# Attention and two expert layers: groups of 512 and 256 tokens in place of 384 and 384 at the start

## The chip, the cores and the metric

One core of a Trainium2 chip. The metric is device time of one execution in microseconds; the kernel before takes 1459.46 us (median of 3 runs, 1459.11 to 1459.53).

## The reference, cut to what matters

```python
# attention: 8 batches x 8 heads x 576 tokens x 64; keys and values pooled by 8 -> 72
k_p = k.reshape(B, H, Sp, 8, D).mean(axis=3)
v_p = v.reshape(B, H, Sp, 8, D).mean(axis=3)
attn = softmax(scale * q @ k_p.T)                  # float32
x = (attn @ v_p) as [4608 tokens, 512]
h = x @ w_in                                       # 512 -> 2048
x2 = (h * cos(h)) @ w_out                          # 2048 -> 512
logits = x2 @ w_gate                               # 8 experts, the best one alone
out[mask_e] = gate * (relu(x2[mask_e] @ w1[e]) @ w2[e])
```

## The kernel before

The 4608 tokens go through attention and the first dense layer in 12 groups (`NG`) of 384 tokens (`GT`), three tiles of 128; then the routed experts follow, which the change leaves alone but for one load. A group g has 16 steps s, one for each 128 of the 2048 hidden features:

- `mm1(s)` (L394): 12 matmuls of 384 columns into one of two banks HB (x and w_in are each a high and a low part: high x high, low x high, high x low). x of the group lies in xTh, xTl.
- `chain_a(s)`: ScalarE scales (L402) and rounds into the bank RB (L403); VectorE takes the rest of the division by 2 pi (L405, a bank and `tA` as inputs); ScalarE takes the sine (L406). `chain_b(s)`: VectorE multiplies with h from its bank (L411), ScalarE copies the high part gh (L412), POOL forms the low part gl (L413).
- `mm2(s)` (L420): 9 matmuls of 512 columns, three for each tile, summed over s in the three banks ACC. It runs two steps late, behind mm1(s+2). mm2(15) stands behind mm1(0) of the next group, and there `evac` copies the three sums to x2t (L425 to L427) and stores them to `x2d` (L429, three DMAs on SP).

Group 0 also decodes the weights, which arrive as raw 64-bit numbers: for each step `w_load` (two DMAs of 512 KB), `w_scale` (two ScalarE operations, L514), `w_bits` (six VectorE operations of 128x512, L519 to L521, through two rotating banks), `w_parts` (two ScalarE casts L526, two POOL subtractions L527), all some steps ahead. In the opening, before the loop, the keys and values of batch 0 are pooled (`pool_k` L313, `pool_v` L324), the three tiles of group 0 get their `scores` (L335, L342 to L348, softmax weights), `norm` (L355 to L358, the last on POOL), `transp` (L365, copies L369 and L371) and `pv` (L382, high part L385 on ScalarE, low part L386 on VectorE), and the first decodes run.

Each later group's attention is hung on the steps of the group before it, by `at(step, function)`: a score at steps 1, 5, 9 (in group 0 at 9, 12, 13), its transposes three steps later, the four pv at the end. So are the pooling of keys and values for the next batch (`load_k`, `pool_k`, `load_v`, `pool_v`), the queries' load two groups ahead (`load_q`, L303, 768 KB), and from group 1 on the routing: 24 `route_dot` (L452) of VectorE for each group on the evacuated x2t, spread over steps 1 to 11, then `route_sel`, `route_pos`, `route_put`.

Nothing is reordered: each engine and each DMA queue works its instructions in the order of the program, and semaphores make it wait. The order within a step of groups 1 to 10 is

```python
mm1(s)
if s == 0: mm2(15)
if s >= 2: mm2(s - 2)
chain_a(s)
if s == 0: evac(g - 1)
route_dot(...)
chain_b(s)
route_dot(...)
for f in ex[s]: f()     # scores, norm, transp, pool_k, load_q, ...
```

and in group 0 the decode of step s+3 stands inside `chain_a(s)`, between L403 and L405, with `chain_b(s-1)` after its second operation.

## Time and profile before

| | |
|---|---|
| median of 3 runs | 1459.46 us |
| profiled execution, its time | 1458.9 us |
| profiled execution, its span | 1457.1 us |
| TensorE busy | 1406.2 us (97%) |
| VectorE, ScalarE, POOL busy | 878.0, 736.3, 442.9 us (60%, 51%, 30%) |
| mm1(0) of group 0, of group 1, of group 2 starts | 32.14, 127.93, 204.87 us |
| TensorE's idle time before L394, ended by VectorE's L411 | 4.8 us in all |

The span runs from the first instruction to the last of the profiled execution; its time holds 1.8 us more. Rows of a timeline give start, duration, engine, line, what is written and read, and in brackets how long the engine was idle before and what ended that. A matmul's duration in a timeline is longer than the distance between two, since they overlap; the distance is what counts. A row of busy time by stretch gives the stretch, then its length and, for PE, PEld (TensorE's weight loads), DVE, ACT and POOL, the busy microseconds with the count of instructions, then the granted clock of TensorE (1.00 being full speed), the share of the DMA engines and their GB/s. DVE is VectorE, ACT ScalarE.

### The profile page before, as it was taken

To read this page: it belongs to the slowest core of one execution; us is meant where nothing else is said; L and a number is where in the kernel's file an instruction comes from. 1 tells how busy PE (TensorE), PEld (TensorE's weight loads), DVE (VectorE), ACT (ScalarE), POOL (GpSimd) and SP (SyncE) were. 2 spreads that over 40 slices of the span, in tenths; PEclk is the share of its full clock that TensorE was granted. 3 is DMA by queue.
4 is the path that set the end of the run, shared out by engine and by line. 5 is a ranking of instruction groups with operands and counts; after the bars stand their busy time and mean duration, and the time that the engine had idled before them with its cause. 6 is when DMAs were issued, how large, how long until landed. Compare 5 with 4: busy or idle time off the path is not lost. (4 is left out here: it accounts for less than half of the span.)

```text
span 1457.1 us, 23304 instructions
## 1 busy us (share of the span) xinstructions
PE 1406.2 (97%) x8295; PEld 1219.2 (84%) x8295; DVE 878.0 (60%) x1949; ACT 736.3 (51%) x1353; POOL 442.9 (30%) x421
## 2 busy tenths in 40 slices
...
GB/s 301 201 149 110 63 47 63 38 2 22 71 39 63 47 23 22 55 55 39 63 30 23 22 1 82 59 37 211 213 233 210 146 156 157 32 44 42 59 30 32
DMA packets 42692, 119.94 MB, mean 82 GB/s; under 512 B 6179, under 2 KB 22179, under 8 KB 39856
## 3 DMA queue, kind: packets, MB, share of 16 engines
...
## 5 line engine op out<-in xcount | busy, mean ns | idle before, releaser
L394 PE MATMUL bank<-xh,WI 128*128 128x384 f32 x1536 | 436.5, 345 | 6.5 <-DVE tA L411 4.8
L420 PE MATMUL bank<-wb,gh 128*128 128x512 f32 x1152 | 395.8, 398 | 0.0
L394 PEld LDWEIGHTS bank<-xh,WI 128*128 128x128 f32 x1536 | 284.6, 190 | 19.5 <-DVE tA L411 7.0
L420 PEld LDWEIGHTS bank<-wb,gh 128*128 128x128 f32 x1152 | 217.2, 189 | 53.5 <-issue 5.3
L394 PE MATMUL bank<-xl,WI 128*128 128x384 f32 x768 | 260.9, 340 | 0.2 <-DVE xl L386 0.2
L420 PE MATMUL bank<-wb,gl 128*128 128x512 f32 x576 | 228.3, 396 | 0.3 <-POOL gl L413 0.2
L807 PEld LDWEIGHTS bank<-E,wb 128*128 128x128 f32 x1632 | 208.7, 191 | 20.0 <-issue 7.4
L807 PE MATMUL bank<-E,wb 128*128 128x256 f32 x1632 | 213.9, 283 | 5.3 <-DVE xh L811 2.5
L452 DVE SCALAR_TENSOR_TENSOR E<-x2t,wgb 128x512 bf16<-128x512 f32 x264 | 216.6, 820 | 2.1
L817 PE MATMUL bank<-wb,xh 128*128 128x512 f32 x816 | 209.5, 395 | 0.0
L810 ACT ACTIVATE xh<-bank 128x256 fp32r<-128x256 f32 x136 | 52.2, 384 | 293.8 <-PE bank L807 293.8
L811 DVE SCALAR_TENSOR_TENSOR xh<-bank,xh 128x256 fp32r<-128x256 f32 x136 | 57.5, 424 | 217.3 <-ACTq L995 96.5
L413 POOL TENSOR_TENSOR gl<-tA,gh 128x384 fp32r<-128x384 f32 x96 | 107.7, 1122 | 252.5 <-ACT gh L412 245.9
L413 POOL TENSOR_TENSOR gl<-E,gh 128x384 fp32r<-128x384 f32 x96 | 105.3, 1097 | 260.3 <-ACT gh L412 224.1
L817 PEld LDWEIGHTS bank<-wb,xh 128*128 128x128 f32 x816 | 145.5, 189 | 25.4 <-issue 0.2
L394 PEld LDWEIGHTS bank<-xl,WI 128*128 128x128 f32 x768 | 146.5, 191 | 4.8 <-DVE xl L386 0.5
L196 POOL DMA_INDIRECT E<-x2d,E x44 | 46.1, 1048 | 271.2 <-PE bank L631 256.8
L420 PEld LDWEIGHTS bank<-wb,gl 128*128 128x128 f32 x576 | 108.6, 189 | 18.6 <-POOL gl L413 1.0
L405 DVE SCALAR_TENSOR_TENSOR tA<-bank,tA 128x384 f32<-128x384 f32 x96 | 52.8, 550 | 77.9 <-ACT bank L403 77.9
L405 DVE SCALAR_TENSOR_TENSOR E<-bank,E 128x384 f32<-128x384 f32 x96 | 53.1, 553 | 61.7 <-ACT bank L403 61.6
L406 ACT ACTIVATE E<-E 128x384 f32<-128x384 f32 x96 | 50.4, 525 | 72.3 <-DVE E L405 72.0
L402 ACT ACTIVATE tA<-bank,consts 128x384 f32<-128x384 f32 x96 | 55.1, 574 | 52.0 <-PE bank L394 52.0
...
## 6 DMA issues: line engine op xcount, KB each, us to landing
...
```

The source lines that it names most:

```text
L196: POOL.indirect_dma_start(out=xg[i], out_offset=None, in_=x2d[0:n], in_offset=bass.IndirectOffsetOnAxis(ap=column(u, i)[0], axis=0), bound ...
L394: PE.matmul(o, lhsT=a, rhs=x[:, c], start=n == 0, stop=n == 11)
L402: ACT.activation(a, h, AF.Identity, scale=INV2PI, bias=consts[:, C_TP + 1:C_TP + 2])
L405: DVE.scalar_tensor_tensor(a, r, MAGIC, a, op0=ALU.subtract, op1=ALU.subtract)
L406: ACT.activation(a, a, AF.Sin, scale=-TWOPI)
L413: POOL.tensor_tensor(gl[s % 2], a, gh[s % 2].bitcast(F32), op=ALU.subtract)
L420: PE.matmul(ACC[i], lhsT=a[:, sl], rhs=w_tile(s)[:, DM * w:DM * w + DM], start=s == 0 and n == 0, stop=s == NCH - 1 and n == 2)
L452: DVE.scalar_tensor_tensor(junk, x2[i], 1.0, wgb[:, DM * e:DM * e + DM], op0=ALU.mult, op1=ALU.mult, accum_out=lgs[:, i, e:e + 1])
L807: PE.matmul(o, lhsT=w_tile(4 * w + s // 2)[:, f], rhs=x[:, c], start=n == 0, stop=n == 11)
L810: ACT.activation(h, o, AF.Relu)
L811: DVE.scalar_tensor_tensor(l, o, 0.0, h.bitcast(F32), op0=ALU.max, op1=ALU.subtract)
L817: PE.matmul(OP[i], lhsT=a[s % 3][:, 128 * i:128 * i + 128], rhs=w_piece(w, s), start=s == 0 and n == 0, stop=s == 7 and n == 2)
```

## The change

Group 0 takes four tiles (512 tokens) and group 1 two (256); the others keep three. `WIDTH`, `BEGIN` and `TILES` replace `GT` where a group's tokens are counted. What follows from it:

- the fourth sum of group 0 goes to the bank ROT[0], and waits there until the end of group 1: `evac(0)` takes three tiles, `evac(1)` takes ROT[0] and group 1's two. The rotating banks are RB and ROT[1] in group 0, ACC[2] and ROT[1] in group 1;
- the rounding of chain_a goes in group 0 to SBUF (`kin`), no longer to the bank RB, since that bank rotates;
- x of group 0 (channel block 3), and gl of odd steps, lie in a new tile X0; its place is taken later by QF, the queries of group 2 and on. So `load_q(2)` stands in group 1, step 0, behind `evac(0)`; `load_q(1)` moves from the opening to group 0, step 4;
- group 0's queries and softmax weights use weight places and EF; the opening has a fourth score, norm and transp; the four `pv(0, c)` all stand ahead of `w_scale(2)` and `w_bits(2)`, no longer between its operations;
- one score and two transposes fewer stand in group 0; the pooling of values for batch 2 (`load_v`, `pool_v`) moves from group 1, steps 5 to 14, to group 2, steps 0 to 5;
- the first expert's w1 is loaded in two DMAs (EF and QF).

```diff
+BEGIN = [0, GT + TP] + [GT * g for g in range(2, NT // GT + 1)]
+WIDTH = [b - a for a, b in zip(BEGIN, BEGIN[1:])]
+TILES = [w // TP for w in WIDTH]
...
+    X0 = ep.tile([128, 4 * GT], F32R, name="X0", tag="e2")
+    Q0 = [w_tmp(i) for i in range(2)] + [EF[:, 2 * W0 * i:2 * W0 * i + 2 * W0] for i in range(3)] + [w_tmp(2)]
...
+    def xT(g, k, c):
+        t, w = (xTh, xTl)[k].rearrange("p c t -> p (c t)"), WIDTH[g]
+        if g == 0 and c == 3:
+            return X0[:, W0 * k:W0 * k + W0]
+        return t[:, w * c:w * c + w]
...
+    def gx(g, k, p):
+        w = WIDTH[g]
+        if g == 0:
+            return X0[:, 2 * W0:] if k and p else GB[:, W0 * (2 * p + k):W0 * (2 * p + k) + W0]
...
+    def accs(g):
+        return ACC + ROT[0:1] if g == 0 else ACC[0:TILES[g]]
...
-    def chain_a(s, meanwhile=lambda: None):
-        h, r = HB[s % 2][:, 0:GT], RB[:, 0:GT]
-        a = tA[s % 2]
+    def chain_a(g, s, meanwhile=lambda: None):
+        h, a = HB[s % 2][:, 0:WIDTH[g]], tA(g, s % 2)
+        r = kin[:, 0:W0] if g == 0 else RB[:, 0:WIDTH[g]]
...
     def evac(g):
         for i in range(3):
+            acc = (ROT[0:1] + ACC if g == 1 else ACC)[i]
...
     w_load(4)
-    pv(0, 0)
+    for c in range(4):
+        pv(0, c)
     w_scale(2)
-    w_bits(2, {2 * i: lambda i=i: pv(0, i) for i in (1, 2)})
-    pv(0, 3)
+    w_bits(2)
     w_parts(1)
...
-            for i in range(3):
+            for i in range(TILES[g + 1]):
                 if g == 0:
-                    at((9, 12, 13)[i], scores, 3 * (g + 1) + i, i)
-                    at((9, 12, 13)[i], norm, i)
-                    if i < 2:
-                        at((11, 14)[i], transp, i)
+                    at((9, 12)[i], scores, g + 1, i)
+                    at((9, 12)[i], norm, i)
+                    at((11, 14)[i], transp, g + 1, i)
...
-            if g + 2 < NG:
-                at(10 if g > 0 else 14, load_q, g + 2)
+            if 0 < g < NG - 2:
+                at(10, load_q, g + 2)
+            if g == 0:
+                at(4, load_q, 1)
...
+        if g == 2:
+            for c in range(4):
+                at((0, 2, 3, 5)[c], pool_v, 2, c)
+                if c < 3:
+                    at((0, 2, 3)[c], load_v, 2, c + 1)
...
             if s == 0 and g > 0:
                 evac(g - 1)
+                if g < 3:
+                    rbanks[:] = [ACC[2], ROT[1]] if g == 1 else ROT
+                if g == 1:
+                    QF.append(ep.tile([128, 4 * GT], F32, name="QF", tag="e2"))
+                    load_q(2)
```

The order of the instructions at three places. **VectorE in the opening**, from the end of the second decode on; before, L386 is pv's subtraction and L519 to L521 are the decode:

```order
L521 SCALAR_TENSOR_TENSOR tmp_157<-wgb,bank_85 128x512
L386 TENSOR_TENSOR xl<-bank_78,xh 128x384
L519 TENSOR_SCALAR bank_79<-tmp_155 128x512
L519 TENSOR_SCALAR bank_80<-tmp_156 128x512
L386 TENSOR_TENSOR xl<-bank_81,xh 128x384
L520 SCALAR_TENSOR_TENSOR bank_79<-tmp_155,bank_79 128x512
L520 SCALAR_TENSOR_TENSOR bank_80<-tmp_156,bank_80 128x512
L386 TENSOR_TENSOR xl<-bank_82,xh 128x384
```

In the changed kernel (L433 is the subtraction, L565 to L567 the decode):

```order
L567 SCALAR_TENSOR_TENSOR tmp_160<-wgb,bank_79 128x512
L433 TENSOR_TENSOR xl<-bank_80,xh 128x512
L433 TENSOR_TENSOR xl<-bank_81,xh 128x512
L433 TENSOR_TENSOR xl<-bank_82,xh 128x512
L433 TENSOR_TENSOR X_108<-bank_83,X_108 128x512
L565 TENSOR_SCALAR bank_84<-tmp_157 128x512
L565 TENSOR_SCALAR bank_85<-tmp_158 128x512
```

The four subtractions, spread through the decode before, stand in a row ahead of it.

**SP at the start of group 1**, before (L303 loads queries, L765 the gate weights, L429 stores the evacuated tiles, L309 and L319 load keys and values):

```order
L319 DMA wgb<-vP 72x1024 x4
L303 DMA early<-qT 128x4x384
L765 DMA wgb<-wgt 128x4096
L429 DMA x2d<-x2t 128x512 x3
L309 DMA E_71<-kT 128x576 x3
```

In the changed kernel (L343, L827, L475 and L349 are the same loads and stores):

```order
L359 DMA wgb<-vP 72x1024 x4
L827 DMA wgb<-wgt 128x4096
L475 DMA x2d<-x2t 128x512 x3
L343 DMA QF<-qT 128x4x384
L349 DMA E_71<-kT 128x576 x4
```

The queries of group 2 move from ahead of the gate weights to behind the three stores.

**VectorE in group 2**, step 2 of the changed kernel to L456 of step 3 (L450 and L456 are L405 and L411 of before, L498 the dots, L364 pool_v, L353 pool_k):

```order
L450 SCALAR_TENSOR_TENSOR TA<-bank_83,TA 128x384
L498 SCALAR_TENSOR_TENSOR E_72,lgs<-x2t,wgb 128x512
L456 TENSOR_TENSOR TA<-bank_78,TA 128x384
L498 SCALAR_TENSOR_TENSOR E_72,lgs<-x2t,wgb 128x512 x2
L522 TENSOR_REDUCE st_117<-sm_114 128x3
L523 TENSOR_SCALAR st_117<-st_117 128x3
L524 RECIPROCAL pay<-st_117 128x3
L364 TENSOR_REDUCE E_71<-E_71 72x128
L353 TENSOR_REDUCE E_71<-E_71 128x72
L450 SCALAR_TENSOR_TENSOR E_72<-bank_83,E_72 128x384
L498 SCALAR_TENSOR_TENSOR E_72,lgs<-x2t,wgb 128x512
L456 TENSOR_TENSOR E_72<-bank_79,E_72 128x384
```

The L364 row is new there; the other rows stand as they did.

## Rows read from the trace of the kernel before

**Rows 1.** Busy time by stretch, three stretches of groups 0 and 1.

```profile
43.00:46.00 3.00, 3.00 (x10) 3.00 (x11) 3.00 (x6) 2.88 (x6) 2.54 (x3) 0.50 0.13 31
50.00:60.00 10.00, 10.00 (x53) 9.20 (x52) 10.00 (x19) 9.63 (x19) 8.01 (x8) 1.00 0.60 210
128.00:205.00 77.00, 77.00 (x427) 66.67 (x428) 58.73 (x133) 48.55 (x83) 21.51 (x19) 1.00 0.16 52
```

**Rows 2.** Timeline of TensorE, group 0 and the start of group 1.

```profile
42.83 0.69 PE L394 MATMUL bank<-xh,WI 128*128 128x384 f32 x1 [4.50 <-DVE tA L411]
...
82.39 0.44 PE L335 MATMUL bank<-E,early 64*128 64x72 f32 x2 [2.25 <-DVE x2t L521]
...
127.93 0.44 PE L394 MATMUL bank<-xh,WI 128*128 128x384 f32 x1
```

**Rows 3.** Timeline of TensorE, one full step of group 0 at full speed.

```profile
53.93 0.34 PE L394 MATMUL bank<-xh,WI 128*128 128x384 f32 x1
...
56.02 0.39 PE L420 MATMUL bank<-wb,gh 128*128 128x512 f32 x1
...
58.11 0.34 PE L394 MATMUL bank<-xh,WI 128*128 128x384 f32 x1
```

**Rows 4.** Timeline of TensorE, 256-wide matmuls in the experts' part.

```profile
1013.66 1.59 PE L807 MATMUL bank<-E,wb 128*128 128x256 f32 x12
...
1015.09 1.55 PE L817 MATMUL bank<-wb,xh 128*128 128x512 f32 x6
```

**Rows 5.** Timeline of ScalarE, one head's exponential of a score in the opening.

```profile
12.87 0.32 ACT L348 ACTIVATE att<-bank,mxs 128x72 f32<-128x72 f32 x1
```

**Rows 6.** Timeline of VectorE, opening: decodes of weights and pv's subtractions.

```profile
22.72 1.27 DVE L519 TENSOR_SCALAR bank<-wgb 128x512 uint32<-128x512 uint32 x2
...
30.05 0.55 DVE L386 TENSOR_TENSOR xl<-bank,xh 128x384 fp32r<-128x384 f32 x1
...
35.66 1.29 DVE L519 TENSOR_SCALAR bank<-wgb 128x512 uint32<-128x512 uint32 x2
```

**Rows 7.** Timeline of TensorE, opening: pv of group 0.

```profile
26.82 5.39 PE L382 MATMUL bank<-early,E 72*64 72x384 f32 x16
```

**Rows 8.** Timeline of VectorE, group 0: L405 of two neighbouring steps.

```profile
50.91 0.55 DVE L405 SCALAR_TENSOR_TENSOR tA<-bank,tA 128x384 f32<-128x384 f32 x1
...
55.42 0.55 DVE L405 SCALAR_TENSOR_TENSOR E<-bank,E 128x384 f32<-128x384 f32 x1
```

**Rows 9.** Timeline of SP's queue, group 1: stores of group 0, load of queries.

```profile
133.27 1.31 SPq L429 DMA_DIRECT2D x2d<-x2t  x3
...
173.34 0.38 SPq L303 DMA_DIRECT2D early<-qT  x1
```

**Rows 10.** Busy time by stretch: the load's last bytes (last two columns).

```profile
176.00:178.00 2.00, 2.00 (x11) 1.68 (x10) 1.93 (x5) 1.95 (x3) 0.72 (x1) 1.00 0.63 237
```

**Rows 11.** Timeline of VectorE, group 1.

```profile
137.42 0.45 DVE L342 TENSOR_REDUCE mxs<-bank 128x4 f32<-128x288 f32 x1
...
141.65 1.47 DVE L452 SCALAR_TENSOR_TENSOR E<-x2t,wgb 128x512 bf16<-128x512 f32 x1
...
143.53 0.67 DVE L452 SCALAR_TENSOR_TENSOR E<-x2t,wgb 128x512 bf16<-128x512 f32 x1
...
164.89 1.21 DVE L324 TENSOR_REDUCE E<-E 72x128 f32<-72x1024 f32 x1
...
185.59 0.08 DVE L452 DVE_READ_ACCUMULATOR E<-x2t,wgb 128x1 f32 x1
```

**Rows 12.** Timeline of VectorE, group 2.

```profile
208.46 0.56 DVE L405 SCALAR_TENSOR_TENSOR tA<-bank,tA 128x384 f32<-128x384 f32 x1 [4.05 <-ACT bank L403]
...
219.96 0.56 DVE L411 TENSOR_TENSOR tA<-bank,tA 128x384 f32<-128x384 f32 x1
```

**Rows 13.** Timeline of TensorE, group 2: mm1(4).

```profile
220.75 0.34 PE L394 MATMUL bank<-xh,WI 128*128 128x384 f32 x1
```

**Rows 14.** Timeline of POOL, group 0: one of the weights' low parts.

```profile
50.20 1.30 POOL L527 TENSOR_TENSOR WI<-tmp,WI 128x512 fp32r<-128x512 f32 x1
```

More of the change, by code (lines that the diff above doesn't have):

```diff
@@ L241, in split @@
             if isinstance(st, int):
-                s = EF if half == 0 else wgb
+                s = wgb if half else QF[0] if c > 5 else EF
             else:
@@ L376, in pv, with mm1 @@
             hh = 2 * c + h
[L377 to L378 removed]
+            t = BEGIN[g]
+            while t < BEGIN[g + 1]:
                 b = t // S
[L380 to L381 removed]
+                e = min((b + 1) * S, BEGIN[g + 1])
+                sl = slice(t - BEGIN[g], e - BEGIN[g])
                 PE.matmul(o[64 * h:64 * h + 64, sl], lhsT=vp[b % 2][:, hh * D:hh * D + D],
[L383 removed]
+                          rhs=attnT(g, hh)[:, sl], start=True, stop=True)
                 t = e
[L385 to L389 removed]
+        h, l, o = xT(g, 0, c), xT(g, 1, c), o[:, 0:WIDTH[g]]
+        ACT.copy(h, o)
+        DVE.tensor_tensor(l, o, h.bitcast(F32), op=ALU.subtract)
+    def mm1(g, s):
+        o = HB[s % 2][:, 0:WIDTH[g]]
         n = 0
@@ L406, in chain_a, with chain_b, mm2 @@
         ACT.activation(a, a, AF.Sin, scale=-TWOPI)
-    def chain_b(s):
-        h = HB[s % 2][:, 0:GT]
-        a = tA[s % 2]
-        DVE.tensor_tensor(a, h, a, op=ALU.mult)
-        ACT.copy(gh[s % 2], a)
-        POOL.tensor_tensor(gl[s % 2], a, gh[s % 2].bitcast(F32), op=ALU.subtract)
-    def mm2(s):
-        h, l = gh[s % 2], gl[s % 2]
-        for i in range(3):
+    def chain_b(g, s):
+        o, a = HB[s % 2][:, 0:WIDTH[g]], tA(g, s % 2)
+        h, l = (gx(g, k, s % 2) for k in range(2))
+        DVE.tensor_tensor(a, o, a, op=ALU.mult)
+        ACT.copy(h, a)
+        POOL.tensor_tensor(l, a, h.bitcast(F32), op=ALU.subtract)
+    def mm2(g, s):
+        h, l = (gx(g, k, s % 2) for k in range(2))
+        for i, acc in enumerate(accs(g)):
             sl = slice(i * TP, i * TP + TP)
             for n, (a, w) in enumerate(((h, 0), (l, 0), (h, 1))):
-                PE.matmul(ACC[i], lhsT=a[:, sl], rhs=w_tile(s)[:, DM * w:DM * w + DM], start=s == 0 and n == 0, stop=s == NCH - 1 and n == 2)
+                PE.matmul(acc, lhsT=a[:, sl], rhs=w_tile(s)[:, DM * w:DM * w + DM], start=s == 0 and n == 0, stop=s == NCH - 1 and n == 2)
     def evac(g):
         for i in range(3):
+            acc = (ROT[0:1] + ACC if g == 1 else ACC)[i]
             if i == 1:
-                DVE.tensor_copy(x2[i], ACC[i])
+                DVE.tensor_copy(x2[i], acc)
             else:
-                ACT.copy(x2[i], ACC[i])
+                ACT.copy(x2[i], acc)
             r = (3 * g + i) * TP
@@ L568, in w_parts @@
                 p.parts()
[L570 removed]
+    seed = TA[:, 0:288].rearrange("p (r two) -> p r two", two=2)
     POOL.memset(seed[:, :, 0], SENT)
@@ L575, in attention_moe_kernel @@
         load_k(0, c)
-    for i in range(3):
-        t = slice(i * TP, i * TP + TP)
-        SP.dma_start(out=qs[:, :, t], in_=qT[:, :, t].rearrange("c p t -> p c t"))
+    for t in (slice(0, TP), slice(TP, W0)):
+        for i in range(2):
+            SP.dma_start(out=Q0[i].rearrange("p (c t) -> p c t", c=2)[:, :, t], in_=qT[2 * i:2 * i + 2, :, t].rearrange("c p t -> p c t"))
     for c in range(4):
@@ L594, in attention_moe_kernel @@
     pool_v(0, 0)
-    scores(1, 1, True)
+    scores(0, 1, True)
     norm(0, True)
     pool_v(0, 1)
-    scores(2, 2)
+    scores(0, 2)
     norm(1, True)
+    scores(0, 3, True)
+    w_scale(0)
     norm(2)
-    w_scale(0)
+    norm(3, True)
     pool_v(0, 2)
```

143 lines of the change are left out of this document (79 added, 64 removed).

## Prediction

> **What bounds the kernel now.** I read the busy time by stretch first, then the timelines of the stretches that the change touches. In group 1 TensorE is busy 77.00 us of 77.00 and VectorE 58.73; in the middle of group 0 VectorE is busy without a gap, 10.00 of 10.00 [rows 1]. So the fourth tile is put where VectorE is the limit, and taken from where TensorE is. A microsecond that TensorE waits in the short group is paid in full; the room in group 0 is what TensorE now loses there. Its timeline shows that: a wait of 4.50 us before mm1(2) at 42.83, one of 2.25 at 82.39 [rows 2], and smaller ones up to the group's end. Behind the first the granted clock is 0.50, the lower of the two levels, from 43 to 46 us and on [rows 1].
>
> **Widths.** Twelve 384-wide matmuls of mm1 take 2.09 us (53.93 to 56.02) and nine of mm2 as long (to 58.11): 4.18 a step [rows 3], 0.174 and 0.233 each. Twelve 256-wide ones elsewhere take 1.43 (1013.66 to 1015.09), 0.119 each [rows 4]. mm2's matmuls are 512 wide, so mm1's at 512 get their 0.233. A step then costs TensorE 12 x 0.233 + 12 x 0.233 = 5.59 with four tiles and 12 x 0.119 + 6 x 0.233 = 2.83 with two. 192 x (0.233 + 0.119 - 2 x 0.174) = 0.8 us more than 384 twice; it is inside the steps below.
>
> **Opening.** The fourth tile needs its softmax before the loop: eight exponentials on ScalarE of 0.3, 2.4 us [rows 5]; on VectorE two more maxima and three small operations, about 1.0, and 1.5 of waiting for ScalarE. The first weight decode, at 22.72 [rows 6], starts near 25.2 and ends at 28.9. The fourth tile's transposes use its banks, so the last of their copies end near 31.1. pv's 16 matmuls take 5.39 us for 384 columns [rows 7]; by proportion 7.2 at 512, and I take 6.9: until 38.0. Before, VectorE's four subtractions L386 stood between the operations of decode 2, and it never waited: the first at 30.05, decode 3 at 35.66 [rows 6]. Now all four stand ahead of decode 2, each behind its pv; the last ends near 39.35, decode 2 takes 3.6 (35.66 - 30.05 less four L386 of 0.47, as before), and decode 3 starts at 43.0. From there to mm1(2) it was 7.2 us (35.66 to 42.83: the decode, L405, two pool_k, two operations of decode 4, L411); with 512 columns 0.2 more. mm1(2) starts at 50.4, not 42.83: **+7.5**. Bounds: pv at full speed, 16 x 0.233 = 3.7, leaves +4.3; a collision of VectorE with POOL adds 0.7.
>
> **Rest of group 0.** VectorE repeats every 4.51 us (50.91 to 55.42) [rows 8]: six decode operations, 3.58, and two of 0.47. At 512 columns those two come to about 0.6 each: 4.78, under TensorE's 5.59. So TensorE becomes the limit and its waits from 82 us on go; the one before mm1(2) stays, and with it the slow stretch, which lost half of 5.8 us, 2.9. Counted forward on TensorE: 14 steps of 5.59 are 78.3; mm2(14) 2.8; the slow stretch 2.9. Scores, transposes and pv of a group of three are what group 1 has over its steps, 77.0 - 16 x 4.18 = 10.1; of two tiles, 6.7. What is late next: transposes at step 11 want a bank that a decode still holds, about 1.5, and mm2(14) its last gl, about 0.7. Together 92.9, where 85.1 stood (42.83 to 127.93 [rows 2]): +7.8, for a tile that adds 14 x (5.59 - 4.18) = 19.7. Group 1 begins at 50.4 + 92.9, say 143.
>
> **Group 1, two tiles.** Two things hold it. First, the queries of group 2. Their new place is that of x and gl of group 0, free only after mm2(0,15), and the load stands on SP behind the three stores of the evacuation. Their issue ended at 133.27 + 1.31 = 134.6 [rows 9], 4.6 after mm1(0) (127.93 + 2.09). With narrower ScalarE operations ahead of it I take 4.0: 143 + 1.43 + 4.0 = 148.4. Such a load takes 4.0 us from its issue at 173.34 [rows 9] to its last bytes, which fall between 176 and 178 [rows 10]; it lands at 152.4. Before, it was issued in group 0 and cost nothing. TensorE has mm1(0), mm2(0,15) and mm1(1) to do, 1.43 + 2.8 + 1.43, and stands before the first score from 148.7: 3.7 us idle, then slow.
>
> Second, VectorE. Steps 1 to 11 of the old group took it 48.2 us, from the first score to the last dot (137.42 to 185.59): 24 dots, mostly of 0.68, and 1.47 beside POOL's normalization [rows 11], and three scores with their waits for exp. Of this 2.7 were waits for TensorE, 2.4 two pool_v of 1.21 [rows 11], which leave; 2.8 go with 128 columns fewer in 21 operations. That is 40.3; I take **41**, with a collision more. TensorE's part of these steps is 11 x 2.83, and 4.4 of the 10.1: 35.5. So VectorE sets the pace, and with two HB banks TensorE can be two steps ahead and no more. The first score reaches VectorE at 154.2, and step 12 starts at 195.2. Behind it 19.3 us stood (185.59 to 127.93 + 77.0), less four narrower steps and a shorter mm2(14), 6.1. Group 2 starts at 208.4, not 204.9: **+3.5**. Its mm2(1,15) has 6 matmuls and not 9: **-0.7**.
>
> **Group 2** now has four pool_v of 1.21, at steps 0, 2, 3 and 5. The first falls into idle time, 4.05 before L405 at 208.46. The others stand ahead of an L411 with little slack: that of step 2 ended at 219.96 + 0.56 = 220.5 [rows 12], and mm1(4), which needs it, began at 220.75 [rows 13]. Three times 1.21, less such slack and VectorE's own waits there: **+2.1**; bounds 0 and 3.6. The last group's first weight load goes out in two pieces, one issue of 0.4 more [rows 9] on a queue that TensorE doesn't wait for there: nothing.
>
> **Sum**: +3.5 - 0.7 + 2.1 = +4.9 on the profiled execution (1458.9 us, 0.6 below the median): 1463.8, or 1464.5 beside the median of 1459.46. Opening and group 0 are inside the +3.5, since they set where group 1 begins.
>
> **Operands in SBUF.** In group 0 L405 now reads two operands from SBUF; its rounding buffer leaves the bank. The row with a bank has 0.55 [rows 8] while POOL is busy (1.30 at 50.20 [rows 14]). The dots, which read two from SBUF, take 1.47 beside POOL's normalization and 0.67 without it [rows 11]. So L405 could wait up to 1.30 for a POOL instruction; if each did, VectorE's step would be 4.78 + 1.30 = 6.08, over 5.59. [...]
>
> **Rivals.**
> A, faster: group 1 runs at TensorE's pace, as before. For it: VectorE's share there was 58.73/77. The group is then 77.0 less 16 x 0.66 of mm1 and 15 x 0.70 of mm2, plus 0.7 for mm2(0,15): 56.6 from 143, so 199.6, 8.8 less than forecast; and group 2's pool_v hide: 1464.5 - 8.8 - 2.1 = 1453.6. It is decided by whether VectorE needs more than 35.5 for steps 1 to 11. Against it: those steps were dense, with 2.7 of waits in 48.2, and the load can't start sooner. 0.17.
> B, no change: only the load holds group 1, or only VectorE, 3.7 or 5 less; or pv in the opening runs at full speed, 3.2 less: 1458 to 1462. 0.27.
> C, far slower: L405 waits in most steps of group 0: 6.08 - 5.59 = 0.49 in 10 steps, 5 more: 1469.5. For it the dots; against it POOL idles in a third of each step, and 0.8 is to spare. 0.12.
> D, the change does less than it says: VectorE still sets group 0, and the wait at 82.39 comes back with a slow stretch, 2.25 + 2.7: 1469.4. 0.06.
>
> **Numbers.** The forecast keeps 0.38. The range, 1453 to 1470, takes in A, C and the bounds of group 2. Outside lie a fast opening together with A, C together with D, and small waits summed on either side: 2 in 10. The forecast's own range is 1461 to 1468. A measurement of this kernel can tell 0.2% (2.9 us) from nothing: faster is below 1456.5, slower above 1462.4. Faster: A and a little of B, 0.2. Same: most of B, 0.25. Slower: the rest, 0.55.
>
> **What would show it.** mm1(2) at 50; no wait over 1.5 us of TensorE between 60 and 130; VectorE busy 4.8 of each 5.6 there; group 1 from 142 to 145; a wait of 3 to 4 us before its first score, with the queries' bytes just ahead; then waits of TensorE that end with L411; in group 2 the same behind pool_v. L405 of group 0 at 0.6, or at over 1 beside POOL if C is at work. I am wrong if TensorE is busy throughout group 1, or if mm1(2) starts before 47.

## The result and the profile after

The changed kernel takes 1472.05 us (median of 4 runs, 1469.86 to 1473.37) against 1459.33 (4 runs): ratio 1.0083 [1.0069, 1.0096], **12.7 us slower**. The forecast was 1464.5, slower, and its range ended at 1470. The profiled execution is the slowest of the four (1473.37 us, span 1471.6), 14.5 above the span of before.

| us | before | after | forecast |
|---|---|---|---|
| mm1(0) of group 0 | 32.1 | 38.5 | 38.0 |
| mm1(2) of group 0 | 42.8 | 51.9 | 50.4 |
| group 1 (first mm1) | 127.9 | 148.1 | 143 |
| group 2 | 204.9 | 216.3 | 208.4 |
| group 3 | 281.8 | 294.4 | 286.7 |
| group 11, the last | 895.7 | 909.9 | - |
| from there to the end | 561.4 | 561.7 | - |

Read downwards: 20.2 us late at group 1, of which the short group gives back 8.8; 12.6 at group 3; and another 1.5 behind that (groups 3 to 10 take 615.5 and not 614.0), where nothing of the work differs.

Busy time by stretch of the kernel after (columns as in [rows 1]): group 0 in its middle, group 1, four pieces of group 1, and groups 3 to 10.

```profile
60.00:80.00 20.00, 20.00 (x88) 16.18 (x87) 20.00 (x28) 15.56 (x28) 15.55 (x12) 1.00 0.57 184
148.00:216.00 68.00, 60.78 (x385) 50.71 (x384) 48.57 (x129) 41.49 (x84) 17.42 (x19) 0.95 0.18 57
158.50:161.00 2.50, 2.45 (x19) 2.35 (x20) 0.68 (x2) 0.00 (x0) 0.00 (x0) 0.56 0.02 6
161.00:164.00 3.00, 3.00 (x14) 2.81 (x13) 2.14 (x6) 1.38 (x3) 0.00 (x0) 0.50 0.00 0
165.00:166.00 1.00, 1.00 (x6) 0.81 (x6) 0.89 (x2) 0.98 (x2) 0.34 (x1) 0.67 0.00 0
166.00:168.00 2.00, 2.00 (x15) 1.82 (x15) 1.94 (x6) 1.10 (x3) 0.92 (x1) 1.00 0.00 0
295.00:910.00 615.00, 615.00 (x3503) 536.49 (x3502) 444.47 (x1040) 384.92 (x664) 197.60 (x184) 1.00 0.12 36
```

In the middle of group 0 both engines are now full, 20.00 of 20.00: TensorE's step rose to VectorE's, as forecast, but VectorE's rose too. Group 1, which was TensorE's without a gap, has it idle for 7.2 us of 68, and behind the wait for the first score the granted clock is 0.56 from 158.5 to 161 and 0.50 from 161 to 164; it is 0.67 from 165 to 166 and 1.00 from 166 on.

TensorE's waits (timeline):

```profile
51.86 0.79 PE L441 MATMUL bank<-xh,WI 128*128 128x512 f32 x1 [5.57 <-DVE att L456]
...
100.81 0.27 PE L377 MATMUL bank<-E,early 64*64 64x72 f32 x1 [1.69 <-DVE x2t L567]
...
101.40 0.27 PE L377 MATMUL bank<-E,early 64*64 64x72 f32 x1 [0.26 <-DVE x2t L567]
...
108.59 0.50 PE L441 MATMUL bank<-xh,WI 128*128 128x512 f32 x1 [0.69 <-DVE E L456]
...
116.06 1.23 PE L405 MATMUL bank<-consts,tmp 128*72 128x128 f32 x8 [1.59 <-DVE E L567]
...
144.22 2.58 PE L465 MATMUL bank<-wb,GB 128*128 128x512 f32 x10 [0.83 <-POOL GB L458]
...
158.55 1.77 PE L375 MATMUL bank<-E,QF 64*128 64x72 f32 x16 [4.59 <-DMA QF<-qT]
...
182.22 0.38 PE L441 MATMUL bank<-xh,WI 128*128 128x256 f32 x1 [0.25 <-DVE TA L456]
...
197.45 0.39 PE L441 MATMUL bank<-xh,WI 128*128 128x256 f32 x1 [1.03 <-DVE TA L456]
...
207.93 0.39 PE L441 MATMUL bank<-xh,WI 128*128 128x256 f32 x1 [0.80 <-DVE E L456]
```

Against [rows 2]: the wait before mm1(2) grew from 4.50 to 5.57. Of the room in group 0, 1.69 at 100.81 and 1.59 at 116.06 came back, both ended by a weight decode (L567). In group 1 the first score waited 4.59 for its queries, which SP had issued at 153.59, behind the stores:

```profile
152.17 1.32 SPq L475 DMA_DIRECT2D x2d<-x2t  x3
153.59 0.40 SPq L343 DMA_DIRECT2D QF<-qT  x1
```

Three waits of TensorE in group 1 end with L456, in the steps behind a score and at the end. VectorE:

```profile
34.13 0.69 DVE L433 TENSOR_TENSOR xl<-bank,xh 128x512 fp32r<-128x512 f32 x1 [1.27 <-ACT xh L432]
...
35.84 0.69 DVE L433 TENSOR_TENSOR xl<-bank,xh 128x512 fp32r<-128x512 f32 x1 [1.02 <-ACT xh L432]
...
39.25 0.69 DVE L433 TENSOR_TENSOR X<-bank,X 128x512 fp32r<-128x512 f32 x1 [1.02 <-ACT X L432]
...
43.43 1.28 DVE L565 TENSOR_SCALAR bank<-wgb 128x512 uint32<-128x512 uint32 x2
...
47.01 1.70 DVE L450 SCALAR_TENSOR_TENSOR att<-E,att 128x512 f32<-128x512 f32 x1
...
66.74 1.66 DVE L450 SCALAR_TENSOR_TENSOR E<-E,E 128x512 f32<-128x512 f32 x1
...
72.49 1.66 DVE L450 SCALAR_TENSOR_TENSOR att<-E,att 128x512 f32<-128x512 f32 x1
...
116.52 0.68 DVE L450 SCALAR_TENSOR_TENSOR E<-E,E 128x512 f32<-128x512 f32 x1
```

The subtractions L433 wait 1.0 to 1.3 for each pv, so decode 3 starts at 43.43 (43.0 forecast; [rows 6] had 35.66). L450 of group 0, the old L405, takes 1.37 to 1.70 in 13 of 16 steps, with 1.66 the commonest, where [rows 8] had 0.55 at 384 columns; in the other three, as at 116.52, it takes 0.68 or 0.69. POOL at these places:

```profile
66.55 1.30 POOL L573 TENSOR_TENSOR WI<-E,WI 128x512 fp32r<-128x512 f32 x1
...
67.81 1.75 POOL L573 TENSOR_TENSOR wb<-E,wb 128x512 fp32r<-128x512 f32 x1
...
115.29 1.29 POOL L458 TENSOR_TENSOR GB<-att,GB 128x512 fp32r<-128x512 f32 x1 [1.71 <-issue]
...
116.53 1.84 POOL L573 TENSOR_TENSOR WI<-tmp,WI 128x512 fp32r<-128x512 f32 x1
```

At 66.74 POOL had begun L573 at 66.55, and L450 ended 0.59 after it did (68.40 against 67.81 by the next start); POOL's next one then took 1.75 and not 1.30. At 116.52 L450 came first and kept its 0.68, and POOL's operation of 116.53 was stretched to 1.84. That is the collision of rival C, in both directions: in these two pairs the first kept its time (POOL's 1.30, L450's 0.68), and the second took longer (L450 1.66, POOL 1.84).

### The profile page after: what moved, and what is told of

Read it like the earlier page. It is cut to its first block, busy times and chain, and to the rows that moved or that the text cites. A ratio compares the mean times of both kernels' runs of the same rounds, so it can differ in the third digit from the quotient of the medians.

```text
span 1471.6 us, 23310 instructions
## 1 busy us (share of the span) xinstructions
PE 1411.2 (96%) x8295; PEld 1213.0 (82%) x8295; DVE 887.5 (60%) x1946; ACT 735.1 (50%) x1371; POOL 448.1 (30%) x421
## 5 line engine op out<-in xcount | busy, mean ns | idle before, releaser
L465 PE MATMUL bank<-wb,GB 128*128 128x512 f32 x1696 | 435.3, 397 | 0.9 <-POOL GB L458 0.8
L441 PE MATMUL bank<-xh,WI 128*128 128x384 f32 (+2 forms) x1504 | 426.2, 346 | 9.5 <-DVE att L456 5.6
L465 PEld LDWEIGHTS bank<-wb,GB 128*128 128x128 f32 x1696 | 315.8, 189 | 72.4 <-ACT xh L432 5.0
L441 PEld LDWEIGHTS bank<-xh,WI 128*128 128x128 f32 x1504 | 276.9, 190 | 27.8 <-DVE att L456 6.5
L441 PE MATMUL bank<-xl,WI 128*128 128x384 f32 (+2 forms) x752 | 255.5, 340 | 0.0
L498 DVE SCALAR_TENSOR_TENSOR E<-x2t,wgb 128x512 bf16<-128x512 f32 x264 | 215.3, 815 | 2.1
L873 DVE SCALAR_TENSOR_TENSOR xh<-bank,xh 128x256 fp32r<-128x256 f32 x136 | 57.5, 424 | 216.3 <-ACTq L1057 94.5
L458 POOL TENSOR_TENSOR GB<-E,GB 128x384 fp32r<-128x384 f32 (+1 forms) x88 | 95.3, 1083 | 246.3 <-ACT GB L457 215.6
L458 POOL TENSOR_TENSOR GB<-TA,GB 128x384 fp32r<-128x384 f32 (+1 forms) x88 | 97.0, 1103 | 235.3 <-ACT GB L457 235.3
L879 PEld LDWEIGHTS bank<-wb,xh 128*128 128x128 f32 x816 | 145.5, 189 | 25.4 <-issue 0.2
L441 PEld LDWEIGHTS bank<-xl,WI 128*128 128x128 f32 x752 | 143.4, 191 | 6.1
L450 DVE SCALAR_TENSOR_TENSOR TA<-bank,TA 128x384 f32<-128x384 f32 (+1 forms) x88 | 47.3, 537 | 76.5 <-ACT bank L448 76.3
L451 ACT ACTIVATE E<-E 128x384 f32<-128x384 f32 (+2 forms) x96 | 50.4, 525 | 77.4 <-DVE E L450 77.2
L450 DVE SCALAR_TENSOR_TENSOR E<-bank,E 128x384 f32<-128x384 f32 (+1 forms) x88 | 47.6, 541 | 60.3 <-ACT bank L448 59.4
L457 ACT CAST GB<-E 128x384 fp32r<-128x384 f32 (+2 forms) x96 | 49.2, 512 | 61.8 <-DVE E L456 59.8
L447 ACT ACTIVATE TA<-bank,consts 128x384 f32<-128x384 f32 (+1 forms) x88 | 49.6, 564 | 45.4 <-PE bank L441 45.4
```

What stands on the lines that cost most here:

```text
L441: PE.matmul(o, lhsT=a, rhs=xT(g, k, c), start=n == 0, stop=n == 11)
L447: ACT.activation(a, h, AF.Identity, scale=INV2PI, bias=consts[:, C_TP + 1:C_TP + 2])
L450: DVE.scalar_tensor_tensor(a, r, MAGIC, a, op0=ALU.subtract, op1=ALU.subtract)
L451: ACT.activation(a, a, AF.Sin, scale=-TWOPI)
L457: ACT.copy(h, a)
L458: POOL.tensor_tensor(l, a, h.bitcast(F32), op=ALU.subtract)
```

## Experiments

All are compared with the kernel before on the same chip. Group starts are read from each trace. Traces of kernels with one and the same opening differ (after, e2, e4, e6, e19): mm1(0) of group 0 comes at 37.4 to 38.5, its first L450 takes 0.71 to 1.70, mm1(2) comes at 49.8 to 51.9 and group 1 at 145.5 to 148.1. The profiled execution of the change is the last of them each time. So starts that differ by less than 3 us show little by themselves; the lengths of groups repeat better. Medians in us; what each kernel was to the kernel before:

| run | median | ratio, interval | mm1(2) | group 1 | group 2 | group 3 |
|---|---|---|---|---|---|---|
| after | 1472.05 | 1.0083 [1.0069, 1.0096] | 51.9 | 148.1 | 216.3 | 294.4 |
| e2_q_early | 1468.06 | 1.0063 [1.0047, 1.0080] | 50.4 | 146.6 | 210.4 | 288.5 |
| e11_before_late_q | 1468.04 | 1.0058 [1.0039, 1.0077] | 42.8 | 128.2 | 213.1 | 289.9 |
| e6_q_early_half_dots | 1468.08 | 1.0058 [1.0041, 1.0074] | 50.1 | 145.5 | 207.1 | 285.2 |
| e5_before_r_sbuf | 1463.50 | 1.0033 [1.0022, 1.0044] | 43.2 | 133.7 | 210.7 | 287.6 |
| e1_r_bank | 1474.57 | 1.0104 [1.0083, 1.0125] | 51.3 | 147.0 | 216.5 | 294.6 |
| e15_act3 | 1474.47 | 1.0105 [1.0088, 1.0122] | 50.7 | 146.4 | 215.1 | 293.4 |
| e3_inter | 1469.09 | 1.0067 [1.0050, 1.0084] | 49.7 | 145.2 | 213.7 | 292.1 |
| e12_before_order | 1460.71 | 1.0009 [0.9999, 1.0019] | 44.3 | 129.5 | 206.5 | 283.4 |
| e4_pvback | 1471.11 | 1.0079 [1.0062, 1.0096] | 49.8 | 146.1 | 215.9 | 292.4 |
| e9_q_inter | 1473.56 | 1.0051 [1.0035, 1.0066] | 48.6 | 143.9 | 207.7 | 285.8 |
| e10_q_inter_spread | 1464.72 | 1.0044 [1.0027, 1.0060] | 48.5 | 142.5 | 206.7 | 284.8 |
| e16_q_inter_act3 | 1468.63 | 1.0067 [1.0050, 1.0085] | 50.5 | 146.1 | 209.9 | 288.2 |
| e17_norm_late | 1469.18 | 1.0067 [1.0050, 1.0083] | 51.0 | 145.3 | 211.6 | 289.8 |
| e21_q_inter_pad64 | 1463.05 | 0.9974 [0.9963, 0.9986] | 49.1 | 142.3 | 206.0 | 284.3 |
| e22_before_pad128 | 1457.81 | 0.9946 [0.9929, 0.9964] | 42.9 | 127.3 | 203.5 | 279.7 |

e9 and e18 to e22 ran on another chip, where the kernel before takes 1466.2 to 1466.5; their ratios stand against that. In their traces the part from group 11's start to the end takes 567 to 571 us, against 560 to 563 elsewhere (568 in e6, whose routing is another). e18 to e20 ran once each (1466.67, 1471.80, 1470.80); of them only the stretches of the trace are read.

### The load of the queries

**e2_q_early**: the changed kernel; X0 in two tiles, the high part of x's last block apart.

```diff
+    X3 = ep.tile([128, 4 * TP], F32R, name="X3", tag="e3")   # its place is QA's later
+                at(15, load_q, 2, (0,))                      # g == 0: tile 0's queries into QA
-                    load_q(2)
+                    load_q(2, (1,))                          # tiles 1 and 2, as before
```

> The changed kernel, but the queries of group 2's first tile have a place of their own, that of the high part of x's last block, and are loaded at step 15 of group 0; the other two tiles' queries load where all did. If the load wait holds group 1: the wait of 4.59 us before the first score goes, and with it the slow clock from 158.5 to about 166 (4 us more); group 2 starts 8.5 us sooner, about 1463.5. If VectorE sets the pace behind it, as I forecast, it takes back 3 to 4 of these in waits of TensorE that end with L456: about 1467. If the load was hidden by other waits: no change, 1472.

Group 1 took 63.8 us (146.6 to 210.4) and not 68.2: the wait for the load is gone and the slow clock with it, 4.5 less (behind the wait at 160.98, below, the 256-wide matmuls start 0.12 apart; at a clock of 0.50, at 160.63 in the change's trace, they start 0.21 apart). The first score reaches VectorE 8.4 us after the group's start and not 12.2, which is 3.8 of it; from there to step 12 VectorE takes 41.6 (155.00 to 196.64) and not 42.3. In place of the wait:

```profile
160.98 0.39 PE L458 MATMUL bank<-xh,WI 128*128 128x256 f32 x1 [1.56 <-DVE TA L473]
...
176.27 0.38 PE L458 MATMUL bank<-xh,WI 128*128 128x256 f32 x1 [1.05 <-DVE TA L473]
...
191.51 0.38 PE L458 MATMUL bank<-xh,WI 128*128 128x256 f32 x1 [1.01 <-DVE TA L473]
...
202.00 0.39 PE L458 MATMUL bank<-xh,WI 128*128 128x256 f32 x1 [0.84 <-DVE E L473]
```

These are four waits for VectorE's L473 (L456 of the change), three of them behind the scores. By the load TensorE lost about 8 us in this group: 4.59 of waiting, and about 3.4 in the 6.8 us at a granted clock of 0.50 (158.8 to 165.7). Its other waits grew from 2.6 to 5.0, so VectorE takes back a good part, as the second theory said.

**e11_before_late_q**: the kernel before, three tiles, `load_q(2)` moved from group 0, step 14, to behind `evac(0)`.

> The kernel before, with one thing of the change: the queries of group 2 are loaded in group 1, step 0, behind the three stores, and not in group 0. If the load is a price by itself: bytes land near 139.5, the first score waits 4 to 5 us for them, and the slow clock behind it costs 3 more: 1466 to 1468. Rival: VectorE and TensorE have other work there, or catch up: under 2 us, 1460 to 1462.

```profile
140.57 1.98 PE L335 MATMUL bank<-E,early 64*128 64x72 f32 x16 [5.80 <-DMA early<-qT]
```

A wait of 5.80, with a granted clock of 0.50 from 140 to 142 and 0.62 from 142 to 146 behind it; group 1 took 84.9 (128.2 to 213.1), 7.9 more than before. So the late load is a price of its own, the largest single one.

**e6_q_early_half_dots**: e2 with 12 of group 1's 24 dots left out.

```diff
+    POOL.memset(lgs, 0.0)
...
-            todo = dots.get(s, [])
+            todo = [n for n in dots.get(s, []) if g != 1 or n % 2 == 0]
```

> As e2_q_early, and group 1 leaves out every second dot of group 0's three tiles (12 of 24; their routing is then another). If VectorE sets group 1's pace once the queries come early: the waits of TensorE that end with L456 in group 1 (5.0 us in e2_q_early) go, group 1 takes 58 to 59.5 us instead of 63.8, about 1463.5. Rival, the waits are those of the chain through ScalarE and POOL: group 1 stays above 62.5, 1467.

Group 1 took 61.7 (145.5 to 207.1), 2.1 less than e2, where some 8 us of dots were left out. The waits behind the scores stayed, the fourth went:

```profile
159.83 0.39 PE L458 MATMUL bank<-xh,WI 128*128 128x256 f32 x1 [1.56 <-DVE TA L473]
...
174.53 0.39 PE L458 MATMUL bank<-xh,WI 128*128 128x256 f32 x1 [1.02 <-DVE TA L473]
...
189.22 0.39 PE L458 MATMUL bank<-xh,WI 128*128 128x256 f32 x1 [1.04 <-DVE TA L473]
```

So neither of the two theories holds: VectorE's sum of work is a part of it, and not the larger one. What makes the waits behind the scores is not shown. One candidate is the score, which stands as one piece of 3.75 us between two steps of 2.83. Another is the dot that follows it, ahead of the L473 for which TensorE waits; both e6 and e10 left it where it was:

```profile
157.79 1.63 DVE L515 SCALAR_TENSOR_TENSOR E<-x2t,wgb 128x512 bf16<-128x512 f32 x1
...
159.36 0.41 DVE L473 TENSOR_TENSOR TA<-bank,TA 128x256 f32<-128x256 f32 x1
```

```profile
157.73 1.15 POOL L415 TENSOR_TENSOR att<-att,rss 128x576 f32<-128x576 f32 x1 [2.50 <-DVE rss L414]
```

It reads two operands from SBUF and starts just behind POOL's normalization: 1.63 and not 0.68 ([rows 11] had 1.47 and 0.67). So up to 0.95 of each wait may be the same collision as L450's (an estimate from 1.63 and 0.68). No run took this dot alone away. (The other routing changes the experts' part, so this run's median isn't read.)

### The rounding in SBUF

**e5_before_r_sbuf**: the kernel before, with the rounding of group 0 in `kin`.

```diff
-        h, r = HB[s % 2][:, 0:GT], RB[:, 0:GT]
+        h, r = HB[s % 2][:, 0:GT], (kin if g == 0 else RB)[:, 0:GT]
```

> The kernel before, three tiles in each group, with one thing of the change: in group 0 the rounding lies in SBUF (kin), so that L405 reads two operands from SBUF. If the wait for POOL is a price by itself: L405 1.4 to 1.6 instead of 0.55 in most of the 16 steps of a group that VectorE sets, 0.9 each, 10 to 14 us: about 1471. Rival: POOL is seldom at work when L405 starts, or TensorE's step hides it: under 2 us, 1460 to 1462.

The line by its forms (min/median/max in ns):

```profile
L405 DVE SCALAR_TENSOR_TENSOR tA<-bank,tA x88: 527/557/559, 137.4 to 966.4; 128x384 f32<-128x384 f32 x88
L405 DVE SCALAR_TENSOR_TENSOR tA<-E,tA x8: 681/1066/1391, 39.5 to 120.9; 128x384 f32<-128x384 f32 x8
L405 DVE SCALAR_TENSOR_TENSOR E<-E,E x8: 541/1058/1426, 45.5 to 128.4; 128x384 f32<-128x384 f32 x8
```

The operation takes 0.56 with a bank and 1.06 with two operands in SBUF, in the same run. Group 1 started at 133.7, 5.8 late, and 4.3 of it reached the end by the medians (4.8 by the ratio). So the operand has a price of its own, under half of what was expected: 0.5 an operation and not 0.9. In a typical step L405 started at 61.79, when POOL's operation of 1.30 had run for 0.65 (from 61.14), so that, by my estimate, only the rest of it stood in the way.

**e1_r_bank**: the changed kernel with the rounding in RB, and the decode on one rotating bank.

```diff
-        r = kin[:, 0:W0] if g == 0 else RB[:, 0:WIDTH[g]]
+        r = RB[:, 0:WIDTH[g]]
...
-            ops = [f for ab in zip(a, b) for f in ab]
+            ops = a + b if k > 2 else [f for ab in zip(a, b) for f in ab]
```

> The changed kernel, but in group 0 the rounding goes to the bank RB again, so that L450 reads one operand from SBUF; the decode uses the other rotating bank alone, its two halves one behind the other. If the two SBUF operands cost (L450 1.6 us beside POOL, 13 times): L450 back to 0.68, mm1(2) at 50.9 instead of 51.86, VectorE's step in group 0 4.8 instead of 5.75, and the waits of TensorE at 100.8 and 116.1 shrink; group 1 starts 3 to 4 us sooner, about 1468.5. Rival, the long L450 is hidden under TensorE's 5.59 but for the first: about 1471.

L450 was 0.69 in all steps, yet group 1 started at 147.0, within the spread of the traces, and nothing reached the end (1.0104 against 1.0083). The edit brought its own costs: decode operations that follow each other on one bank start 0.73 and 0.80 apart, not 0.60, and the transposes that share RB waited for L450:

```profile
114.50 1.07 PE L405 MATMUL bank<-consts,tmp 128*72 128x128 f32 x8 [3.10 <-DVE E L450]
```

**e15_act3**: the same aim without a bank: ScalarE takes off the constant, L450 reads h from its bank.

```diff
+        if g == 0:
+            ACT.activation(r, r, AF.Identity, bias=kon[:, 0:1])
+            meanwhile()
+            DVE.scalar_tensor_tensor(a, r, -TWOPI, h, op0=ALU.mult, op1=ALU.add)
+            ACT.activation(a, a, AF.Sin, bias=kon[:, 1:2])
+            return
```

> The changed kernel; in group 0 ScalarE also takes the large constant off the rounded value (a third operation on each step), and L450 computes h - 2 pi r from the bank of h and one operand in SBUF, the quarter turn going into the sine's bias. If the two SBUF operands beside POOL are the price: L450 0.68 in all steps, VectorE's step 4.8, ScalarE's 5.3, both under TensorE's 5.59; the waits at 100.8 and 116 get short, group 1 starts 3 to 5 us sooner, about 1468. Rival, the long L450 is hidden, or ScalarE becomes the limit instead: group 1 starts within 1 us of before, 1471 to 1473.

```profile
L455 DVE SCALAR_TENSOR_TENSOR att<-E,bank x8: 678/683/687, 46.7 to 133.4; 128x512 f32<-128x512 f32 x8
L455 DVE SCALAR_TENSOR_TENSOR E<-E,bank x8: 673/683/689, 53.0 to 140.4; 128x512 f32<-128x512 f32 x8
```

The long operation is gone and the wait at 100.8 with it; group 1 began at 146.4, again within the spread. But ScalarE (the fourth busy time) is now nearly full beside TensorE, and VectorE no longer:

```profile
60.00:80.00 20.00, 20.00 (x87) 16.09 (x87) 16.85 (x28) 19.11 (x33) 14.35 (x12) 1.00 0.55 182
```

The waits of group 0 behind mm1(2) were 3.9 us, against 5.1 in the change's trace and 3.5 in e4's, so they are no shorter than with the long operation; and groups 3 to 10 took 617.0 us (below). In sum the collision is shown in the operation's duration, three ways. In the changed kernel it costs up to 1 us before mm1(2): from mm1(0) to mm1(2) it is 13.3 us where the first L450 takes 1.70 (after) and 12.4 where it takes 0.71 (e4). Behind mm1(2) TensorE's 5.59 covers all but 0.16 of VectorE's 5.75 in a step, and e1 and e15 are 0.5 shorter than the change from mm1(2) to group 1 (95.7 against 96.2), with the costs of their own edits in it. What the long L450 costs there by itself was not separated.

### The opening

**e3_inter**: the changed kernel with pv between the operations of decode 2, as it stood in the kernel before.

```diff
-    for c in range(4):
-        pv(0, c)
+    pv(0, 0)
     w_scale(2)
-    w_bits(2)
+    w_bits(2, {2 * i: lambda i=i: pv(0, i) for i in (1, 2)})
+    pv(0, 3)
```

> The changed kernel, but with pv(0,1) and pv(0,2) between the operations of decode 2 and pv(0,3) behind it, as before. If the order in the opening costs what I forecast (VectorE waits 4.3 us between the four subtractions, from 32.9 to 39.9): decode 3 starts at 40.0 instead of 43.43, mm1(2) at 48.4 instead of 51.86, and 3 us of it reach the end: about 1469. Rival, TensorE's own cold matmuls of mm1(0) and mm1(1), or ScalarE, set mm1(2): less than 1 us, 1471.5.

```profile
40.46 1.29 DVE L565 TENSOR_SCALAR bank<-wgb 128x512 uint32<-128x512 uint32 x2 [0.68 <-ACT wgb L560]
...
49.74 0.79 PE L441 MATMUL bank<-xh,WI 128*128 128x512 f32 x1 [3.62 <-DVE att L456]
```

Decode 3 started at 40.46 and mm1(2) at 49.74, 11.6 us after mm1(0); the traces with the change's opening have 12.4 to 13.3 there, e9 and e10, with this order too, 11.2 and 10.8. So the order costs 1 to 2 us, and not all of the 2.9 by which group 1 starts sooner than in the change's trace. By the ratios the run is 2.3 us shorter, but the two intervals overlap. The rival was not run by itself; in the change's trace the granted clock was 0.50 in mm1(0) (38.5 to 42.5, its matmuls 0.43 from start to start) and 1.00 in mm1(1) (43 to 47, 0.23). **e12_before_order** is the reverse in the kernel before:

> The kernel before, with one thing of the change: all four pv of group 0 ahead of decode 2. If the order in the opening is a price by itself: VectorE waits 3 to 4 us between the four subtractions, mm1(2) at 46 to 46.5 instead of 42.83, and since VectorE sets group 0, all of it reaches the end: 1462.5. Rival, the decodes have slack in the opening: under 1 us.

```profile
44.31 0.69 PE L394 MATMUL bank<-xh,WI 128*128 128x384 f32 x1 [5.76 <-DVE tA L411]
```

There mm1(2) came at 44.31 and not 42.83, 1.5 late and not 3 to 4, and the interval of the time reaches 1: with three tiles the order costs 1.5 us by the trace, and by the time no more than the interval allows, 0.2%.

### pool_v

**e4_pvback**: `load_v` and `pool_v` of batch 2 back in group 1, steps 5 to 14.

> The changed kernel, but with load_v and pool_v of batch 2 back in group 1, steps 5 to 14. If pool_v costs group 2 what its time rose by: group 2 gets 1.2 us shorter; if VectorE sets group 1's pace from step 2 on, the four pool_v add 2 to 4 us there: 1473.5 to 1475. Rival, VectorE has room in group 1 once TensorE was late and slow anyway: group 1 as long as now, 1471.

Group 2 took 76.5 (215.9 to 292.4), 1.6 less; group 1 69.9, 1.6 more. Moving it neither won nor lost.

### Together

**e9_q_inter** has e2's and e3's edits; **e10_q_inter_spread** also spreads group 1's dots; **e16_q_inter_act3** has e2's, e3's and e15's; **e17_norm_late** is e16 with group 1's norms a step later. Of the lines, the first is e10's and the other two are e17's.

```diff
+            for s, k in enumerate((0, 4, 4, 4, 4, 4, 4) if last else (0, 0, 2, 3, 1, 0, 3, 3, 1, 0, 3, 3, 2, 3) if g == 1 else (0, 1, 3, 3, 2, 1, 3, 2, 2, 1, 2, 4)):
...
-                    at(1 + 4 * i, norm, i)
+                    at((2 if g == 1 else 1) + 4 * i, norm, i)
```

> The changed kernel with the early queries, pv between the operations of decode 2, and the dots of group 1 spread over steps 2 to 13 with none in the steps of a score (route_sel at 13). If the costs are separate and add: 4.4 and 2.9 less as each alone, and 2 to 3 of the 5.0 us of waits in group 1: 1462 to 1463. Rival, what one gives back the next takes (the opening's gain is lost in waits of group 0 for VectorE): 1466.

> The changed kernel with the early queries and with pv between the operations of decode 2, dots as in the change. If the two add and the spread dots of e10 gained nothing: 1464 to 1465. Rival, the spread dots were worth the 2 us that they were meant to be: 1466 to 1467.

> The changed kernel with all three undone: early queries, pv between the operations of decode 2, and L450 with one operand in SBUF. If these three prices are all that stands between the fourth tile and a gain: 4.4 + 2.9 + 3 to 4 less, 1461, and about the time of the kernel before. Rival, they overlap (what one gives the next wait takes): 1464 to 1465, as with two of them.

> As e16_q_inter_act3, and in group 1 the norm of each score stands one step later, so that VectorE's score of 3.75 us is cut in two (2.0 and 1.2) and doesn't wait for the exponential. If the waits of 1.5, 1.0 and 1.0 us in group 1 come from the one long score in a step of 2.83 us, and not from VectorE's sum of work: they shrink to half, group 1 gets 1.5 to 2.5 us shorter. Rival, VectorE's sum sets the pace: the waits move to other steps, group 1 as long as in e16_q_inter_act3.

Group 3 starts at 285.8 (e9) and 284.8 (e10), 8.6 and 9.6 before the change's; e2 and e3 alone had 5.9 and 2.3, so load and order add. Group 1 took 63.7 and 64.1: the spread gained nothing in it, and route_pos then waited 2.33 for the later selection. e16 is worse than either: group 1 comes at 146.1 and not 143.9, a loss that lies before mm1(2) and goes with ScalarE's third operation, the rival; another 1.5 us are lost in groups 3 to 10 (below). In e17 the waits of 1.55, 0.99 and 1.01 became 1.19, 0.64 and 0.64, and new ones came up (0.3 to 0.7, before transposes and scores): group 1 took 66.3 instead of 63.8. So the shorter piece shortens the wait behind it by 0.36, and the group isn't won by it. With all three undone four tiles are still 6.4 us behind the kernel before at group 3's start (288.2 against 281.8).

### The places in SBUF

Groups 3 to 10 do the same in both kernels with TensorE busy all the time, yet take 614.0 us before, 615.5 after, and 617.0 in e15 and e16. The matmuls by line, in the stretch 282 to 896 of before and 294 to 910 of after (busy us, mean ns of one):

```profile
L394 PE MATMUL bank<-xh,WI 128*128 128x384 f32 x1025 | 287.9, 341 | 0.0
...
L420 PE MATMUL bank<-wb,gh 128*128 128x512 f32 x768 | 263.5, 397 | 0.0
```

```profile
L441 PE MATMUL bank<-xh,WI 128*128 128x384 f32 x1025 | 289.3, 343 | 0.0
```

L394 and L441, mm1, take 341 against 343 ns. The change gives two small tables a fourth row, which moves the weights WI and all other tiles that lie behind them up by 64 bytes; e15 and e16 move them by 96. **e18**, **e20** and **e22** add only an unused tile to the kernel before, **e19** to the changed one, **e21** to e9.

```diff
+    p1.tile([128, 16], F32, name="pad")       # 18 in e20 (72 bytes, which take up 96), 32 in e22
```

> The kernel before with an unused tile of 64 bytes, so that the weights WI and all tiles behind them lie 64 bytes higher, as in the changed kernel; no instruction differs. If the places cost the 1.6 us: groups 3 to 10 take 615.5 us, not 613.9, and the run 1.6 to 2 us more. Rival, the instructions' order costs it: 613.9.

> The kernel before with an unused tile of 72 bytes, so that WI lies 96 bytes higher, as in e15_act3 and e16_q_inter_act3 (617.0 us for groups 3 to 10). If the places decide: 617.0. Rival: 613.9.

> The changed kernel with an unused tile of 64 bytes, so that WI lies 128 bytes higher than before the change. If the places decide by their remainder of 128: groups 3 to 10 take 613.9 us, 1.6 less. Rival, the order of instructions, or the places of x in the other pool: 615.5 still.

| WI above its place in before | order of before | changed order |
|---|---|---|
| 0 bytes | 614.0 (before, e5), 613.9 (e11), 613.8 (e12) | - |
| 64 | 615.5 (e18) | 615.5 (after, e1 to e4, e9), 615.4 (e6), 615.7 (e10) |
| 96 | 617.0 (e20) | 617.0 (e15, e16, e17) |
| 128 | 608.1 (e22) | 608.1 (e19, e21) |

In these runs the time of groups 3 to 10 goes by the place alone, whatever the order. At 64 and 96 bytes both chips give the same. e19 was expected to give the 1.5 back; it gave 7.4.

> The kernel before with an unused tile of 128 bytes, so that WI and all behind it lie at the places of e19. If the place alone decides: groups 3 to 10 take 608 us instead of 613.9, and with groups 1, 2 and 11 the run 6 to 8 us less than the kernel before, which would leave four tiles without a gain. Rival, it is the place together with the order or with x in the other pool: 613.9 to 615.6.

> The changed kernel with the early queries, pv between the operations of decode 2, and an unused tile of 64 bytes as in e19. If the prices add: group 3 starts near 285 as in e9 and groups 3 to 10 take 608.1 us, 7 us less than e9 and 1 to 2 us less than the kernel before on the same chip. Rival, the gain of the place was peculiar to e19: as e9, 5 us over the kernel before.

```profile
L421 PE MATMUL bank<-wb,gh 128*128 128x512 f32 x768 | 260.2, 393 | 0.0
```

With 128 bytes it is mm2's matmuls that got shorter, 393 ns against 397. **e22 is the fastest version: 0.9946 [0.9929, 0.9964] of the kernel before, about 8 us less**, with three tiles everywhere. e21, four tiles with load, order and place mended, is 0.9974, ahead of the kernel before but 5.2 us behind e22, at the same place. So the place is no merit of four tiles; at equal place they lose.

## Why the prediction was wrong

The sign was right, and the size was +4.9 where the trace has +14.5 and the runs +12.7. The step that failed is the rest of group 0: the forecast put VectorE's step at 4.78 us, under TensorE's 5.59, and so allowed TensorE 2.2 us of waits there; VectorE's step was 5.75 and the waits 5.1. Group 1's terms were each sized too small, by 2.8 together, and the places of the tiles, 1.5, were no term at all. By the forecast's own terms:

- **Opening, +7.5 to mm1(2): measured 9.0 in this trace.** Decode 3 came at 43.43 for 43.0. (The rows give 3.7 for decode 2, where the sum takes 3.6; it changes nothing.) The rest is L450's first collision, 1.70 for 0.6 (47.01), which stood as a bound of 0.7 and not in the sum. In the other traces with this opening that operation takes 0.71 to 1.05 and mm1(2) comes at 49.8 to 50.4, for 50.4: there the term was right.
- **Rest of group 0, 92.9: measured 96.2.** TensorE's step was 5.6 as forecast. The term that failed is "what is late next", 2.2: the waits were 1.69, 0.26, 0.69, 1.59 and 0.83, 5.1 in all. Four of the five end with VectorE, whose step of 5.75 left it no room to get ahead. That step was put at 4.78 because L405 was put at 0.6 with two operands in SBUF. But the short L450 alone does not mend it: where ScalarE or the sharing of a bank took L450's part (e15, e1), the waits changed their cause and stayed, and from mm1(2) to group 1 it took 94.0 to 96.2 in every variant of the change but e21 (93.2). What would take these waits away stays open.
- **Group 1, 65.4: measured 68.2.** Both things that hold it were right, and both were sized too small. The first score reached VectorE 12.2 us after the group's start, for 11.2: from the load's issue to the score it took 5.0 us (153.59 to 158.55) and not 4.0, and the wait was 4.59 for 3.7. VectorE took 42.3 us from the first score to step 12 (160.29 to 202.58), summed as 41; the rest took 13.7 for 13.2. The slow clock after the wait, which the sum leaves out, is not what was missing: without the wait and without the slow clock VectorE takes 41.6 (e2). The mechanism was put too simply all the same. With 8 us of VectorE's dots left out the group is only 2.1 shorter (e6), so VectorE's sum alone doesn't set it; what stands between a score and L456 does a part, and whether that is the score or the stretched dot behind it was not separated.
- **Group 2, +1.4 with mm2(1,15): measured 1.2.** Right, but not a loss of the move: in group 1 the four pool_v cost the same (e4).
- **After group 3: nothing forecast, 1.5 measured.** The places in SBUF (e18). No row of the trace of before could have shown it.
- **Rival C was priced on top of a group that already ran at TensorE's pace.** That L450 would collide was right: 13 of 16 steps. 5 us for it in group 0 is more than any run of the changed kernel shows; alone in the kernel before, where VectorE sets the pace, it is 4.3 (e5). The dots showed it in the trace of before (1.47 against 0.67 [rows 11]), and L450 in those steps (1.37 to 1.70 against 0.68 and 0.69). I gave the rival too low a chance: POOL was busy 8.01 us of 10 there [rows 1], where I wrote that it idles for a third of the step, so the likely case was the collision.

Where the expected gain went: the room in group 0 was real, waits of 2.25, 1.64 and 1.05 and slow stretches. Three parts of the change, each put alone into the kernel before, cost 8.5 (load), 4.8 (operand) and 1.3 us (order, with an interval that reaches nothing) by their ratios, 14.6 together, and the places 1.5; the whole change costs 12.1 by its ratio. By that sum the fourth tile itself would gain some 4 us, but the prices don't carry over: load and order undone in the changed kernel gave back 4.7 by the ratios (e9), where alone they cost 9.8. No run shows a gain of four tiles. With load and order mended and at the same place (e21 against e22) they lose 5.2. At group 3's start the two traces are 4.6 apart: e21 is 15.1 late at group 1 (6.2 at mm1(2), 8.9 from there on), gains 12.5 in the short group and loses 2.1 in group 2. The collision, the waits of group 1 (5.0 us in e2, 4.5 of them for L456) and the longer opening are still in it; how much each is of the 5.2 was not separated.

Not tried: a rounding bank for group 0 without a cost elsewhere (the kernel's eight banks are taken), the short group at another place, and group 1 without the dot right behind each score.
